# A new order of the loading phase, first weight columns as fp32 on the hardware queue, attention weights transposed by DMA

## The chip, the cores and the metric

The kernel runs on one core of one Trainium2 chip. A core has five engines with a queue of instructions each: PE (TensorE, matmuls; its weight loads are listed as PEld), DVE (VectorE), ACT (ScalarE), POOL (GpSimd) and SP (SyncE, which here only issues DMAs). Instructions of one engine start in order; between engines they wait on semaphores. The metric is the time of one execution on the device in microseconds (us).

## What is computed

Two stages. First a small cross attention between `x` (8 batches, 8 heads, 512 rows, 64 columns) and a `state` of 32 rows per head, in both directions; then a gated linear layer over all rows:

```
scores  = x @ state^T / 8 ;  a  = softmax over the 32 state rows ;  xread = a @ state
scores2 = state @ x^T / 8 ;  a2 = softmax over the 512 rows of x ;  sread = a2 @ x
rows    = concat(xread, sread) with heads side by side          (4352 rows of 512)
out     = (sigmoid(rows @ w_gate) * (rows @ w_val)) @ w_out     (512 -> 1536 -> 512)
```

The kernel never forms `xread`. With SW = state @ w (per batch, for both weights) the first product of the layer is a @ SW, so the normalized attention weights, transposed, go straight into the large matmuls.

## The kernel before

It is written under a manual schedule: the order in which the code issues instructions is the order in each engine's queue.

Names. `xf` is x of a batch in fp32, `xb` in bf16 (two buffers), `xT` its transpose. `sTz` is the state, transposed and padded with zeros so that a pair of heads shares one matmul. `Sp` are the scores in PSUM, `E` their Exp. `rs`, `ri`, `ab` are row sums, reciprocals and normalized weights (`at_norm`, half a batch at a time); `aT` is `ab` transposed: eight PE transposes and a copy on DVE (`at_aT`). `Eb` is E in bf16, cast by POOL, for the other direction (`at_sr`, tiles `srp`, results in `XS`). `sw_visit` makes SW for a range of weight columns in PSUM tiles `swp` (four buffers), and `sw_evac` takes the oldest of them to SBUF, on the engines named. `gv(b, f)` makes 128 gate and 128 val columns of batch b (four matmuls of 512 columns into two `gvp` tiles), then Tanh on ACT (`th`) and the gating product on DVE (`glu`). `out_mm(b, k)` is four matmuls of the last product; every third call ends in a copy to `res` and a store on SP's queue. `warm` issues matmuls without use, to keep PE active.

The program has two phases.

- Loading. State and x of batches 0 and 1 come on SP's queue. The weights, x of batch 2 and `w_out` come on POOL's queue, which casts weights to bf16 on the way; columns 0 to 255 first, then 256 to 511, 512 to 1023, 1024 to 1535. Batches 0 and 1 go through attention (with PE transposes of x), and all 24 of their `gv` are made here, in the hand-written list `order`, with one evacuation on ACT and one on DVE after each entry. The state copies are made in two portions: `sTz` of batches 0 and 1 early, of batches 2 to 7 later, four copies on ACT.
- The loop. In iteration b, step f of twelve issues `out_mm(b-1, f)` and, from b=2 on, `gv(b, f)`. Beside that it prepares batch nb = b+1: SW at steps 0, 4 and 8 with one evacuation a step, scores at steps 2 and 3, `at_norm` at 4 and 5, `at_aT` at 7, `at_sr` at 8. The x of batch nb+1 is cast on POOL and transposed by four DMAs on SP's queue (`at_xT_dma`). There are two `gvp` buffers, so one `gv` is in flight at a time.

An iteration with `gv`, as the code issues it:

```
            if nb is not None:
                if f % 4 == 0:
                    sw_visit(nb, f * 128, 512, 0, 1)
                sw_evac(act)
                ...
                elif f == 4:
                    at_norm(nb, 0, nc.vector)
                    at_Eb(nb)
```

Of the kernel before, what the change touches and what calls it, by code (L numbers as in the profile page):

```python
# [16 lines left out]
def kernel(  # L17
# [58 lines left out]
    def load_w(lo, n):  # L76
        for w, src in ((wg, moe_w_gate), (wv, moe_w_val)):
            nc.gpsimd.dma_start(w[:, :, lo:lo + n], src.rearrange("(k p) n -> p k n", p=128)[:, :, lo:lo + n])
# [16 lines left out]
    def at_xT_pe(b, i, place, cps):  # L95
        ps = place[0].tile((128, 2, 4, 128), BF, name="xTp", tag=place[1])
# [13 lines left out]
    def at_S(b, i, place):  # L110
        if i == 0:
            E1s[b] = ap_.tile((128, 4, 2, 4, Ns), FP, name="E1")
        ps = place[0].tile((128, 4, 2, 2, Ns), FP, name="Sp", tag=place[1])
        for jj in range(2):
            for c in range(4):
                nc.tensor.matmul(ps[:, c, :, jj], xTs[b][:, 2 * i + jj, c], sTz[:, b, 2 * i + jj], start=True, stop=True)  # L116
        nc.scalar.activation(E1s[b][:, :, :, 2 * i:2 * i + 2].rearrange("p c e j n -> p (c e) j n"),  # L117
                             ps.rearrange("p c e j n -> p (c e) j n"), AF.Exp, scale=scale)
# [6 lines left out]
    def at_norm(b, i, eng):  # L125
        if i == 0:
            abs_[b] = ap_.tile((128, 4, 2, 128), BF, name="ab")
        E = E1s[b][:, :, :, 2 * i:2 * i + 2].rearrange("p c e j n -> p (c e) j n")
        rs = ap_.tile((128, 8, 2), FP, name="rs")
        nc.vector.tensor_reduce(rs, E, AX.X, ALU.add)  # L130
        ri = ap_.tile((128, 8, 2), FP, name="ri")
        nc.vector.reciprocal(ri, rs)  # L132
        eng.tensor_tensor(abs_[b].rearrange("p c e (j n) -> p (c e) j n", n=Ns)[:, :, 2 * i:2 * i + 2], E,  # L133
                          ri.unsqueeze(3).to_broadcast((128, 8, 2, Ns)), ALU.mult)

    def at_aT(b, place, cps):
        ps = place[0].tile((128, 2, 4, 128), BF, name="aTp", tag=place[1])
        for e in range(2):
            for c in range(4):
                nc.tensor.transpose(ps[:, e, c], abs_[b][:, c, e], ident)  # L140
        aTs[b] = ap_.tile((128, 2, 512), BF, name="aT")
        m = 2 // len(cps)
        for i, cp in enumerate(cps):
            cp(aTs[b][:, i * m:i * m + m], ps[:, i * m:i * m + m].rearrange("p g c t -> p g (c t)"))

    def at_sr(b, place):
# [7 lines left out]
        for j in range(4):  # L154
            for c in range(4):
                nc.tensor.matmul(sr[:, j], xbs[b][:, c, 2 * j:2 * j + 2].rearrange("p h d -> p (h d)"),  # L156
                                 Eb[:, c, :, j], start=(c == 0), stop=(c == 3))
        r2 = ap_.tile((128, 4, Ns), FP, name="r2")
# [7 lines left out]
    sw_left = []  # L166

    def sw_mm(pss, b, w, lo, n, o):
        for j in range(4):
            for e in range(2):  # L170
                rows = slice(e * 64, (e + 1) * 64)
                nc.tensor.matmul(pss[e][j * Ns:(j + 1) * Ns, o:o + n], sTz[rows, b, j, e],  # L172
                                 (wg, wv)[w][rows, j, lo:lo + n], start=True, stop=True)

    def sw_visit(b, lo, n, *ws):
# [3 lines left out]
        if not ws:  # L179
# [3 lines left out]
            for e in range(2):  # L183
                sw_left.append((SWs[b][:, e, :, lo:lo + n], pss[e].rearrange("p (w n) -> p w n", w=2)))
        for w in ws:
            pss = [p_sw.tile((128, 512), FP, name="swp", tag="swp")[:, :n] for e in range(2)]
            sw_mm(pss, b, w, lo, n, 0)
            for e in range(2):
                sw_left.append((SWs[b][:, e, w, lo:lo + n], pss[e]))

    def sw_evac(*cps):
        for cp in cps:
            if sw_left:
                cp(*sw_left.pop(0))  # L194


    def gv(b, f, place=None):
        place = place or (p_gv, "gv")
# [4 lines left out]
        pss = []
        for w in range(2):
            ps = place[0].tile((128, 512), FP, name="gvp", tag=place[1])[:, :n]
            if b < B:
                for g in range(2):
                    nc.tensor.matmul(ps, SWs[b][:, g, w, fs], aTs[b][:, g], start=(g == 0), stop=(g == 1))  # L208
# [4 lines left out]
        th = fp.tile((128, 512), FP, name="th")[:, :n]  # L213

        nc.scalar.activation(th, pss[0], AF.Tanh, scale=0.5)  # L215
        nc.vector.scalar_tensor_tensor(glus[b][:, f], th, 1.0, pss[1], ALU.add, ALU.mult)  # L216
# [50 lines left out]
    load_x(1, nc.sync)  # L267
    make_identity(nc, ident)
# [154 lines left out]
```

## Time and profile before

| | us |
|---|---|
| median of 3 runs (lowest, highest) | 248.19 (247.83, 249.14) |
| the profiled execution, whole | 247.92 |
| its span | 246.1 |
| loading, to the first output matmul | 53.0 |
| one iteration of the loop, b=2 to 6 | 25.43 |
| busy PE / DVE / ACT / POOL | 229.8 / 128.4 / 139.2 / 36.4 |

All rows of the profile are of that one execution, and times in it count from the start of its span. The row of a stretch gives its borders and length, then busy time and number of instructions of PE, PEld, DVE, ACT and POOL, the clock granted to TensorE (1.00 is full speed), the busy share of the DMA engines and GB/s. The row of a timeline gives start, duration, engine, line, operation, output <- input, and in brackets the idle time before it and what ended that. A row of a group gives its count, busy time and mean duration in ns, and the idle time before it with its releasers. PE's durations overlap: matmuls are pipelined, so the cost of one is the distance from start to start.

### The profile page before, as it was taken

What the parts mean: (1) busy time and instruction counts of PE and PEld (TensorE: products, weight loads), DVE (VectorE), ACT (ScalarE), POOL (GpSimd) and SP (SyncE); (2) the same over time, 40 slices, a digit from 0 to 9 for tenths busy, and PEclk for the clock granted to TensorE, in tenths of its full rate; (3) what the DMA queues carried; (4) which work ended last, traced back from release to release, by engine and by line L of the source; (5) the groups of instructions that cost most, each with busy time, mean ns of one, the idle gap of its engine ahead of it and who ended that gap; (6) DMA issues with size and microseconds to landing.
All of it is one profiled execution on the core that took longest, in us unless ns stands there. A gap on an engine that the chain in (4) does not pass through costs nothing.

```text
span 246.1 us, 4632 instructions
## 1 busy us (share of the span) xinstructions
PE 229.8 (93%) x1828; PEld 114.4 (46%) x1828; DVE 128.4 (52%) x210; ACT 139.2 (57%) x258; POOL 36.4 (15%) x68
## 2 busy tenths in 40 slices
PE   7674999999999999999999999999999999999993
PEld 6651443444544444444443544354445444466643
DVE  2768488965325853485338633854375444332300
ACT  4756367666567556764686467647764734433311
POOL 1796020003304000320013000400020000000000
PEclk9998699999999999999999999999999999999999
DMA  6999996601364516242533444331111111111113
GB/s 226 260 174 207 284 206 78 195 3 43 97 156 176 120 53 187 73 107 64 147 112 87 87 103 153 86 89 45 43 44 45 43 43 43 45 59 69 45 33 96
DMA packets 31734, 25.99 MB, mean 106 GB/s; under 512 B 14048, under 2 KB 27104, under 8 KB 31712
## 3 DMA queue, kind: packets, MB, share of 16 engines
q1 hardware_dynamic: 25488, 19.80, 27.9%
q0 software_dynamic: 6080, 5.77, 13.6%
q8 instruction: 14, 0.23, 0.4%
q10 hardware_dynamic: 144, 0.13, 0.2%
q14 instruction: 8, 0.07, 0.1%
HBM read 18.35 MB, written 8.91 MB: 111 GB/s over the span
## 4 chain that ended last, share of the span: by engine, by line
PE 76%; DVE 13%; issue 4%; ACT 4%; DMA 2%; SPq 0%; ACTq 0%; DVEq 0%
PE outp L229 30%; PE gvp L208 29%; PE swp L172 5%; DVE glu L216 4%; PE gvp L211 4%; DVE rs L130 3%; DVE ab L133 3%; PE srp L153 2%; PE aTp L140 2%; ACT th L215 2%; DMA sf<-in_state_dram 2%; PE srp L156 2%; DVE ri L132 1%; PE Sp L116 1%; ACT E L117 1%
## 5 line engine op out<-in xcount | busy, mean ns | idle before, releaser
L216 DVE SCALAR_TENSOR_TENSOR glu<-th,gvp 128x512 bf16<-128x512 f32 (+1 forms) x108 | 70.9, 656 | 87.7 <-ACT th L215 63.9
L208 PE MATMUL gvp<-aT,SW 128*128 128x512 bf16 x384 | 100.6, 384 | 6.1 <-DVE glu L216 2.5
L229 PE MATMUL outp<-wo,glu 128*128 128x512 bf16 x396 | 100.0, 379 | 0.0
L215 ACT ACTIVATE th<-gvp 128x512 f32<-128x512 f32 (+1 forms) x108 | 61.8, 572 | 59.6 <-PE gvp L208 49.8
L208 PEld LDWEIGHTS <-SW 128*128 128x128 bf16 x384 | 36.7, 98 | 53.1 <-issue 7.9
L229 PEld LDWEIGHTS <-glu 128*128 128x128 bf16 x396 | 36.2, 98 | 41.2 <-issue 4.8
L194 ACT CAST SW<-swp 128x512 bf16<-128x512 f32 (+1 forms) x85 | 48.7, 581 | 7.9 <-PE swp L172 7.1
L233 ACT ACTIVATE res<-outp 128x512 f32<-128x512 f32 x33 | 19.7, 597 | 25.9 <-PE outp L229 23.5
L123 POOL CAST Eb<-E 128x256 bf16<-128x256 f32 x32 | 12.3, 428 | 123.8 <-ACT E L117 123.8
L87 POOL CAST xb<-xf 128x1024 bf16<-128x1024 f32 (+1 forms) x14 | 14.3, 1045 | 19.0 <-PE srp L156 13.0
L133 DVE TENSOR_TENSOR ab<-E,ri 128x512 bf16<-128x512 f32 x16 | 15.8, 989 | 0.5
L130 DVE TENSOR_REDUCE rs<-E 128x16 f32<-128x512 f32 x16 | 10.8, 677 | 4.0 <-ACT E L117 4.0
L172 PE MATMUL swp<-wv,sTz 64*32 64x512 bf16 (+1 forms) x208 | 11.2, 366 | 0.0
L172 PEld LDWEIGHTS <-sTz 64*32 64x32 bf16 x416 | 4.6, 89 | 14.0 <-issue 13.8
L172 PE MATMUL swp<-wg,sTz 64*32 64x512 bf16 (+1 forms) x208 | 10.6, 374 | 0.5 <-DVE glu L216 0.5
L117 ACT ACTIVATE E<-Sp 128x512 f32<-128x512 f32 x16 | 9.8, 613 | 1.5 <-PE Sp L116 1.5
L159 DVE RECIPROCAL r<-srp 128x128 f32<-128x128 f32 x8 | 7.7, 956 | 5.1 <-PE srp L156 5.1
L116 PE MATMUL Sp<-sTz,xT 128*128 128x64 bf16 x128 | 6.5, 193 | 2.5 <-DVE sTz L296 1.1
L116 PEld LDWEIGHTS <-xT 128*128 128x128 bf16 x128 | 5.8, 98 | 6.3 <-DVE sTz L296 1.2
L194 DVE CAST SW<-swp 128x512 bf16<-128x512 f32 (+1 forms) x13 | 8.3, 643 | 0.3 <-PE swp L172 0.2
L262 PE MATMUL warm<-ident 128*128 128x128 bf16 x80 | 7.0, 261 | 1.4 <-POOL ident masks.py:199 1.4
L211 PE MATMUL gvp<-XS,wv 128*128 128x256 bf16 x48 | 7.2, 272 | 0.1
(45 smaller groups left out, 102.0 us busy)
## 6 DMA issues: line engine op xcount, KB each, us to landing
out_dram<-res SPq DMA_DIRECT2D x31, 256.0 KB, 2.3
xf<-in_x_dram SPq DMA_DIRECT2D x6, 1024.0 KB, 6.7
wo<-in_moe_w_out_dram POOLq DMA_DIRECT2D x3, 512.0 KB, 19.0
xf<-in_x_dram SPq DMA_DIRECT2D x2, 512.0 KB, 5.4
wg<-in_moe_w_gate_dram POOLq DMA_DIRECT2D x2, 512.0 KB, 10.3
wv<-in_moe_w_val_dram POOLq DMA_DIRECT2D x2, 512.0 KB, 11.8
xf<-in_x_dram POOLq DMA_DIRECT2D x1, 1024.0 KB, 15.8
sf<-in_state_dram SPq DMA_DIRECT2D x1, 512.0 KB, 3.9
```

What stands on the lines that cost most here:

```text
L87: cp(xbs[b].rearrange("p c h d -> p h c d")[:, lo:lo + n], xfs[b][:, lo:lo + n])
L116: nc.tensor.matmul(ps[:, c, :, jj], xTs[b][:, 2 * i + jj, c], sTz[:, b, 2 * i + jj], start=True, stop=True)
L130: nc.vector.tensor_reduce(rs, E, AX.X, ALU.add)
L133: eng.tensor_tensor(abs_[b].rearrange("p c e (j n) -> p (c e) j n", n=Ns)[:, :, 2 * i:2 * i + 2], E, ri.unsqueeze(3).to_broadcast((128, 8, ...
L172: nc.tensor.matmul(pss[e][j * Ns:(j + 1) * Ns, o:o + n], sTz[rows, b, j, e], (wg, wv)[w][rows, j, lo:lo + n], start=True, stop=True)
L194: cp(*sw_left.pop(0))
L208: nc.tensor.matmul(ps, SWs[b][:, g, w, fs], aTs[b][:, g], start=(g == 0), stop=(g == 1))
L211: nc.tensor.matmul(ps, (wg, wv)[w][:, j, fs], XS[:, j], start=(j == 0), stop=(j == 3))
L215: nc.scalar.activation(th, pss[0], AF.Tanh, scale=0.5)
L216: nc.vector.scalar_tensor_tensor(glus[b][:, f], th, 1.0, pss[1], ALU.add, ALU.mult)
L229: nc.tensor.matmul(ops[b, c], glus[b][:, f, c * 128:(c + 1) * 128], wo[:, f], start=(f == 0), stop=(f == NF - 1))
L233: nc.scalar.activation(res, ops[b, c], AF.Copy, scale=0.5)
```

## The change

It does five things.

1. The loading phase is one flat list of calls with a searched order. For that the helpers are cut into their parts: `xT_mm` and `xT_cp`, `S_mm` and `S_exp`, `n_sum` (sum and reciprocal) and `n_mul` (product), `aT_mm` and `aT_cp`, `sr_mm` and `sr_fin`, `gv_mm`, `gv_th` and `gv_glu`; `sw_cp` evacuates a named tile on a named engine. Two of the four products of loading go to POOL. PE's matmuls of `warm` go from 80 to 56.
2. Columns 0 to 255 of both weights come as fp32 on SP's queue behind x of batch 1 and are cast to bf16 by DVE (gate) and POOL (val). POOL's own loads start after a one-column copy that waits for x of batch 1 (`gate`).
3. The state is cast and copied once, without padding, into `sTc`, from which `sw_visit` now reads; POOL makes `sTz` from it, for batches 1 and 0 early and 2 to 7 at the end of loading.
4. `aT` of batches 2 to 7 is made by four DMA transposes on SP's queue (`aT_dma`) instead of PE and DVE, and its layout is (row block, pair, row), so that PE reads it in four pieces.
5. In the loop, scores are made at steps 0 and 1, sums at 1 and 3, products at 2 and 4, the other direction at 5; x is loaded one batch further ahead.

The core of the diff:

```diff
+    def gate():
+        nc.gpsimd.tensor_copy(pre[:, 1:2], xfs[1][:, 0, 0, 0:1])
+    def cast_w(w, cp):
+        cp((wg, wv)[w][:, :, 0:256], wfs[w])
...
+    def aT_dma(b):
+        for c in range(4):
+            nc.sync.dma_start_transpose(aT_tile(b)[:, c], abs_[b][:, c].rearrange("p e k -> p (e k)"))
...
-                nc.tensor.matmul(pss[e][j * Ns:(j + 1) * Ns, o:o + n], sTz[rows, b, j, e],
+                nc.tensor.matmul(pss[e][j * Ns:(j + 1) * Ns, o:o + n], sTc[rows, b, j],
...
-                    nc.tensor.matmul(ps, SWs[b][:, g, w, fs], aTs[b][:, g], start=(g == 0), stop=(g == 1))
+                    nc.tensor.matmul(ps, SWs[b][:, g, w, fs], aTs[b][:, :, g], start=(g == 0), stop=(g == 1))
...
+    for src in (moe_w_gate, moe_w_val):
+        wf = wp.tile((128, 4, 256), FP, name="wf", bufs=2)
+        nc.sync.dma_start(wf, src.rearrange("(k p) n -> p k n", p=128)[:, :, 0:256])
+        wfs.append(wf)
...
-    sb = wp.tile((128, 16, 2, D), BF, name="sb")
-    nc.vector.tensor_copy(sb[:, :, 0], sf)
-    nc.scalar.copy(sb[:, :, 1], sf)
+    sb = wp.tile((128, 16, D), BF, name="sb")
+    nc.vector.tensor_copy(sb[:, 0:8], sf[:, 0:8])
+    nc.scalar.copy(sb[:, 8:16], sf[:, 8:16])
...
+    def pad(b, n=1):
         for e in range(2):
             rows = slice(e * 64, (e + 1) * 64)
+            nc.gpsimd.tensor_copy(sTz[rows, b:b + n, :, e], sTc[rows, b:b + n])
...
+    sr_mm(0, OU)
+    gv_th(1, 5)
...
+    pad(2, 6)
     cast_x(2, pool, 0, 4)
     cast_x(2, pool, 4, 4)
     at_xT_dma(2)
+    load_x(3, nc.sync)
...
+                lo, q = f // 4 * 512, f % 4
+                if q == 0:
+                    sw_visit(nb, lo, 512, 0, 1)
+                sw_cp(nb, lo, q // 2, q % 2, act)
+                if f < 2:
+                    S_mm(nb, f, AT)
+                    S_exp(nb, f)
                 elif f == 5:
+                    sr_mm(nb, AT)
+                    sr_fin(nb)
...
+                if f in (1, 3):
+                    n_sum(nb, f // 2)
+                elif f in (2, 4):
+                    n_mul(nb, f // 2 - 1, nc.vector)
+                if f == 2:
+                    at_Eb(nb)
+                    if nb + 2 < B:
+                        load_x(nb + 2, nc.sync)
+                elif f == 4:
+                    aT_dma(nb)
```

How the order moves, at three places. First ACT's queue in loading, from the Exp of batch 0's second half on; `E_194` and `E_339` are the Exp tiles of batches 0 and 1. Before:

```order
L117 ACTIVATE E_194<-Sp 128x8x64
L87 CAST xb<-xf 128x4x4x64
L103 COPY xT<-xTp 128x1024
L144 COPY aT<-aTp 128x512
L194 CAST SW<-swp 128x256
L117 ACTIVATE E_339<-Sp 128x8x64
L194 CAST SW<-swp 128x256
L215 ACTIVATE th<-gvp 128x512
L117 ACTIVATE E_339<-Sp 128x8x64
L215 ACTIVATE th<-gvp 128x512
L296 COPY sTz<-stp 64x24x2x8 x4
L194 CAST SW<-swp 128x2x256 x2
```

After, with `E_232` and `E_314` for batches 0 and 1:

```order
L99 CAST xb<-xf 128x4x4x64
L135 ACTIVATE E_232<-Sp 128x8x64
L119 COPY xT<-xTp 128x1024 x2
L135 ACTIVATE E_314<-Sp 128x8x64
L232 CAST SW<-swp 128x256 x2
L135 ACTIVATE E_314<-Sp 128x8x64
L232 CAST SW<-swp 128x256 x2
L232 CAST SW<-swp 128x2x256 x2
L256 ACTIVATE th<-gvp 128x512
L232 CAST SW<-swp 128x2x256 x2
```

The four state copies are gone from ahead of the double-width evacuations, and all evacuations of the first columns are on ACT.

Second, DVE's queue in iteration b=2, which prepares batch 3. Before:

```order
L216 SCALAR_TENSOR_TENSOR glu<-th,gvp 128x512 x5
L130 TENSOR_REDUCE rs<-E_1143 128x16
L132 RECIPROCAL ri<-rs 128x16
L133 TENSOR_TENSOR ab<-E_1143,ri 128x8x64
L216 SCALAR_TENSOR_TENSOR glu<-th,gvp 128x512
L130 TENSOR_REDUCE rs<-E_1143 128x16
L132 RECIPROCAL ri<-rs 128x16
L133 TENSOR_TENSOR ab<-E_1143,ri 128x8x64
L216 SCALAR_TENSOR_TENSOR glu<-th,gvp 128x512 x2
L144 COPY aT<-aTp 128x1024
L216 SCALAR_TENSOR_TENSOR glu<-th,gvp 128x512
L159 RECIPROCAL r_1356<-srp 128x128
```

After:

```order
L261 SCALAR_TENSOR_TENSOR glu<-th,gvp 128x512 x2
L148 TENSOR_REDUCE rs<-E_1111 128x16
L150 RECIPROCAL ri<-rs 128x16
L261 SCALAR_TENSOR_TENSOR glu<-th,gvp 128x512
L156 TENSOR_TENSOR ab<-E_1111,ri 128x8x64
L261 SCALAR_TENSOR_TENSOR glu<-th,gvp 128x512
L148 TENSOR_REDUCE rs<-E_1111 128x16
L150 RECIPROCAL ri<-rs 128x16
L261 SCALAR_TENSOR_TENSOR glu<-th,gvp 128x512
L156 TENSOR_TENSOR ab<-E_1111,ri 128x8x64
L261 SCALAR_TENSOR_TENSOR glu<-th,gvp 128x512
L199 RECIPROCAL r_1268<-srp 128x128
```

A `glu` now stands between each sum and its product, and the copy of `aT` is gone.

Third, SP's queue at the beginning of the loop. Before, after the transposes of batch 2:

```order
L73 DMA xf<-in_x_dram 128x8x256
L235 DMA out_dram<-res 128x512 x2
L108 DMA_TRANSPOSE xT<-xb 128x4x128 x4
L235 DMA out_dram<-res 128x512 x2
L73 DMA xf<-in_x_dram 128x8x256
L235 DMA out_dram<-res 128x512 x2
```

After:

```order
L78 DMA xf<-in_x_dram 128x8x256
L280 DMA out_dram<-res 128x512
L78 DMA xf<-in_x_dram 128x8x256
L177 DMA_TRANSPOSE aT<-ab 128x2x128 x4
L280 DMA out_dram<-res 128x512
L124 DMA_TRANSPOSE xT<-xb 128x4x128 x4
L280 DMA out_dram<-res 128x512 x3
```

Four transposes of `aT` come ahead of the next batch's transposes of x, with one output store between them.

More of the change, by code (lines that the diff above doesn't have):

```diff
@@ L136, in at_aT, with halfE @@
[L136 to L146, printed above, removed]
+    def halfE(b, i):
+        return E1s[b][:, :, :, 2 * i:2 * i + 2].rearrange("p c e j n -> p (c e) j n")
@@ new lines, in aT_mm, with aT_tile, aT_cp @@
+    def aT_mm(b, place):
+        ps = held["aT", b] = place[0].tile((128, 4, 2, 128), BF, name="aTp", tag=place[1])
+        for c in range(4):
+            for e in range(2):
+                nc.tensor.transpose(ps[:, c, e], abs_[b][:, c, e], ident)
+    def aT_tile(b):
+        if b not in aTs:
+            aTs[b] = ap_.tile((128, 4, 2, 128), BF, name="aT")
+        return aTs[b]
+    def aT_cp(b, i, cp):
+        cs = slice(0, 4) if i is None else slice(2 * i, 2 * i + 2)
+        cp(aT_tile(b)[:, cs], held["aT", b][:, cs])
@@ L150, in at_sr @@
-        sm = ps[:, 256:384].rearrange("p (j n) -> p j n", j=4)
+        held["sr", b] = place[0].tile((128, 512), FP, name="srp", tag=place[1])
+        sr, sm = sr_parts(b)
         for e in range(2):
@@ new lines @@
+    xT_cp(0, 1, 1, act)
+    xT_cp(0, 1, 0, vec)
+    cast_x(1, vec, 0, 4)
+    S_mm(0, 0, SWP)
+    S_exp(0, 0)
+    warm(12, SWP)
+    gate()
+    load_w(0, 256, 256)
+    S_mm(0, 1, AT)
+    cast_x(1, act, 4, 4)
+    n_sum(0, 0)
+    xT_mm(1, 0, OU)
+    load_w(1, 256, 256)
+    load_w(0, 512, 512)
+    S_exp(0, 1)
+    cast_w(0, vec)
+    n_sum(0, 1)
+    xT_mm(1, 1, SWP)
+    xT_cp(1, 0, None, act)
+    xT_cp(1, 1, None, act)
+    n_mul(0, 1, nc.vector)
+    S_mm(1, 0, GV)
+    sw_visit(0, 0, 256, 0)
```

332 lines of the change are left out of this document (211 added, 121 removed).

## The prediction

> **What bounds the kernel now.** I read first the page's slices of the granted clock of TensorE, then stretches of the trace cut where the program changes: loading (0 to 53.01), the iteration b=1 (to 67.7) and the five iterations b=2 to 6.
>
> ```profile
> PEclk9998699999999999999999999999999999999999
> ```
> ```profile
> core 0: us, PE busy (x) PEld busy (x) DVE busy (x) ACT busy (x) POOL busy (x), PEclk, DMA share, GB/s
> 16.93:20.84 3.91, 3.27 (x56) 1.29 (x48) 2.24 (x4) 3.46 (x8) 3.40 (x9) 1.00 1.24 206
> 20.84:24.87 4.03, 0.63 (x7) 0.10 (x1) 3.84 (x8) 1.71 (x4) 1.43 (x3) 0.69 1.24 207
> 24.87:29.34 4.47, 4.46 (x31) 1.89 (x32) 1.71 (x3) 1.19 (x2) 0.00 (x0) 0.51 1.14 307
> 29.34:53.01 23.67, 23.67 (x201) 10.19 (x193) 21.10 (x35) 16.27 (x29) 2.02 (x2) 1.00 0.73 138
> ...
> 67.70:194.90 127.20, 124.65 (x964) 57.15 (x963) 68.86 (x109) 81.39 (x152) 15.04 (x28) 1.00 0.34 96
> ```
>
> From 29.34 on PE nearly always has work (23.67 of 23.67 us, then 124.65 of 127.20). Before that it has not: from 20.84 to 24.87 it works 0.63 of 4.03 us, and from 24.87 to 29.34 it works at a granted clock of 0.51. The timeline of that place says why:
>
> ```profile
> 16.43 0.37 ACT L194 CAST SW<-swp 128x256 bf16<-128x256 f32 x1
> ...
> 16.93 0.60 PE L208 MATMUL gvp<-aT,SW 128*128 128x512 bf16 x2
> ...
> 19.57 1.92 ACT L296 COPY sTz<-stp 64x384 bf16<-64x384 bf16 x4
> ...
> 21.52 1.07 ACT L194 CAST SW<-swp 128x512 bf16<-128x512 f32 x2
> ...
> 22.64 0.61 PE L208 MATMUL gvp<-aT,SW 128*128 128x512 bf16 x1 [1.78 <-ACT SW L194]
> 22.93 0.69 DVE L133 TENSOR_TENSOR ab<-E,ri 128x512 bf16<-128x512 f32 x1
> ...
> 23.54 1.28 DVE L194 CAST SW<-swp 128x512 bf16<-128x512 f32 x2
> ...
> 24.88 1.46 PE L208 MATMUL gvp<-aT,SW 128*128 128x512 bf16 x3 [1.62 <-DVE SW L194]
> ...
> 29.34 2.76 PE L208 MATMUL gvp<-aT,SW 128*128 128x512 bf16 x12
> ```
>
> PE waits for evacuations of SW. On ACT they stand behind the state copies (1.92 us), on DVE, busy 3.84 of 4.03 us, behind batch 1's normalization. Between 16.93 and 29.34 only 16 of these matmuls ran, four gv; the fifth gv is the first of the x12 group and ends at about 30.2.
>
> **Part 1, loading.** New are a searched order, the first 256 columns of both weights as fp32 on SP's queue, and state copies without padding. The prices, first from loading, then from the loop:
>
> ```profile
> 0.00:5.00 5.00, 3.64 (x35) 3.65 (x36) 1.28 (x2) 1.85 (x3) 1.04 (x10) 1.00 0.58 193
> 5.00:10.00 5.00, 3.06 (x51) 2.45 (x50) 2.50 (x7) 3.14 (x7) 2.31 (x4) 1.00 1.02 333
> ```
> ```profile
> 7.69 0.61 POOL L87 CAST xb<-xf 128x512 bf16<-128x512 f32 x1 [6.04 <-DMA xf<-in_x_dram]
> ...
> 8.24 0.88 POOL L78 DMA_DIRECT2D wg<-in_moe_w_gate_dram  x1
> ...
> 8.54 0.41 PE L116 MATMUL Sp<-sTz,xT 128*128 128x64 bf16 x8 [1.06 <-DVE sTz L296]
> ...
> 10.77 2.18 DVE L133 TENSOR_TENSOR ab<-E,ri 128x512 bf16<-128x512 f32 x1
> ...
> 11.31 1.09 POOL L87 CAST xb<-xf 128x1024 bf16<-128x1024 f32 x1
> ```
> ```profile
> L208 PE MATMUL gvp<-aT,SW 128*128 128x512 bf16 x48 | 12.6, 379 | 0.6 <-DVE glu L216 0.6
> ...
> L216 DVE SCALAR_TENSOR_TENSOR glu<-th,gvp 128x512 bf16<-128x512 f32 x12 | 8.2, 685 | 10.6 <-ACT th L215 8.6 <-PE Sp L116 1.2 <-PE gvp L208 0.8
> ...
> L194 ACT CAST SW<-swp 128x512 bf16<-128x512 f32 x12 | 7.0, 584 | 0.5 <-PE swp L172 0.4
> ...
> L130 DVE TENSOR_REDUCE rs<-E 128x16 f32<-128x512 f32 x2 | 1.4, 675 | 0.0
> ...
> L116 PE MATMUL Sp<-sTz,xT 128*128 128x64 bf16 x16 | 0.8, 193 | 0.0
> ...
> L156 PE MATMUL srp<-Eb,xb 128*128 128x64 bf16 x16 | 0.6, 193 | 0.0
> ...
> L132 DVE RECIPROCAL ri<-rs 128x16 f32<-128x16 f32 x2 | 0.5, 252 | 0.1
> ```
>
> I walk the new order with such durations, each instruction starting when its engine and its inputs are ready. State and two batches are 2.62 MB; 5 us at 193 GB/s and 5 at 333 make 2.63 MB, so x of batch 1 is there just before 10. The two fp32 blocks (0.52 MB each, 1.6 us at 333 GB/s) land near 11.4 and 13.0.
>
> POOL casts its x until 8.3, then makes four small padded copies (0.25 each, an estimate, well below its cast of 0.61 for four times the columns on twice the partitions), so the first scores start at 9.4 instead of 8.54. It issues three weight loads (0.8 each, to 12.2), normalizes half a batch (`n_mul`) to 13.3 and casts the val block (1.09) to 14.4. ACT carries xT copies, a cast of x and three Exp to 14.7, two evacuations of 256 columns (0.37 each), the fourth Exp and two more evacuations, to 16.75. So the first gv starts at 16.8, as before (16.93): neither the early weights nor the compact copies help that point.
>
> The gain comes right after it. No state copy and no second normalization stands ahead of the evacuations: ACT does two for batch 1, one Tanh (taken like an evacuation, 0.6) and two more by 19.8, DVE two by 20.6. PE runs the second gv at 19.2 and then without long gaps; its fifth gv ends at 22.7, against 30.2. The visits of columns 0 to 511 are done at both points, and what is left is the same: 19 gv, eight half-visits and two sr. That took 53.01 - 30.2 = 22.8 us before. DVE was busy 21.10 of 23.67 us there, so it holds PE back little. Loading then ends at 45.5, 7.5 us earlier.
>
> What the trace of before has no row for is `n_mul` on POOL, with two inputs. Its bounds are 0.61 (POOL's cast of that size) and 2.18 (the slowest product on DVE); I took 1.1, nearer to the cast. The Trainium skill, GPSIMD Engine Reference, Engine selection, says that two-input elementwise work takes about twice as long on GpSimd as on VectorE. By it the price would be an estimated 1.4 us, and the sum 0.3 us worse.
>
> DVE's 2.18 us at 10.77 is mostly a wait beside POOL's DMA issue and cast; the product at 22.93 takes 0.69. The new order puts more POOL work beside DVE, so I take 1.0 us off the walk (0 to 2.5: one or two such waits). **Loading: -6.5 us** (-7.5 to -5.0).
>
> At no cost: the two wide padded copies for batches 2 to 7, which POOL makes while it would be idle (2.02 of 23.67 us busy); and wo, whose 3 MB come last as before and are used only when loading ends.
>
> **Part 2, the loop.** One period of 25.43 us, from 103.50 to 128.93 (the second group of rows above is from it):
>
> ```profile
> 105.11 1.45 DVE L133 TENSOR_TENSOR ab<-E,ri 128x512 bf16<-128x512 f32 x1
> ...
> 106.05 5.14 SPq L108 DMA_TRANSPOSE xT<-xb  x4
> ...
> 109.85 0.61 PE L140 MATMUL aTp<-ident,ab 128*128 128x128 bf16 x8
> ...
> 110.29 1.03 PE L229 MATMUL outp<-wo,glu 128*128 128x512 bf16 x4
> ...
> 111.16 1.03 PE L208 MATMUL gvp<-aT,SW 128*128 128x512 bf16 x4
> ...
> 112.11 0.41 PE L172 MATMUL swp<-wg,sTz 64*32 64x512 bf16 x8
> ...
> 112.67 0.62 PE L153 MATMUL srp<-Eb,ones 128*128 128x128 bf16 x8
> ```
>
> From start to start, eight transposes take 110.29 - 109.85 = 0.44 us of PE, an output step 0.87, a visit 0.56. The transposes leave PE. PE's 0.6 us of waiting for glu comes from sum, reciprocal and product (0.68 + 0.25 + 1.45, the last with POOL's cast beside it) standing together between two glu. Now sum and product stand in different steps: 0.69 + 0.93 and 0.69 + about 0.7 fit into a step of 2 x 0.87 = 1.74 us. POOL's cast can still hold one product; I leave 0.2 us of the wait. So -0.84 a period (-1.04 if nothing is left, -0.4 if the wait stays), five times: **-4.2** (-5.2 to -2.0). DVE's copy of aT goes too, but nothing waited for it.
>
> aT is now read by PE in four pieces instead of one. Of the rows above, S (L116) reads one piece of 64 columns and sr (L156) two of 32: 193 ns both, so nothing is charged.
>
> In SP's queue four aT transposes stand ahead of output stores and of the next xT transposes. An xT issue takes 5.14 / 4 = 1.29 us; aT is half as wide, so between 0.64 and 1.29. Counted from a period's start, the products end at 12.3, aT's issues at most at 17.4, xT's at 22.9, with the landing of the last at about 24.2. The scores need it at 24.6 + 2.4 = 27.0. That leaves 2.8 us, and no charge.
>
> **Part 3, the seam.** The cast and transposes of batch 2 wait for sr of batch 0, which the search put late:
>
> ```profile
> 35.23 2.02 POOL L87 CAST xb<-xf 128x1024 bf16<-128x1024 f32 x2 [12.97 <-PE srp L156]
> ...
> 37.29 6.32 SPq L108 DMA_TRANSPOSE xT<-xb  x4
> ```
> ```profile
> 19.30:22.70 3.40, 1.16 (x34) 0.50 (x33) 2.88 (x6) 3.23 (x7) 2.96 (x8) 0.96 1.24 207
> ```
>
> Cast, issue and about 1.2 us for the last landing take 9.5 us, or 8.4 with issues of 1.29. On PE seven gv (6.1), an output step (0.87) and a visit (0.56), 7.5 us, lie between. So the scores of batch 2, no longer at the third step of b=1 but at the first, wait 0.9 to 2.0 us, which is new. The transposes of aT(2) may also push back xT(3). Against it 0.44 us of transposes go. **Seam: +0.5** (0 to +2).
>
> Sum: -6.5 - 4.2 + 0.5 = -10.2. The profiled execution took 247.92, the median of the runs is 248.19; from the median that is 238.0.
>
> **Rivals.**
> - The clock falls again. Before, it fell late in the last row above, a stretch with 1.16 us of PE work in 3.40, and stayed near 0.5 through 24.87 to 29.34 although PE was full: about 6.8 us in all. The new program drops 24 of 80 warming matmuls, and its work from 10 to 19 us is short pieces. If 6.8 us of dense work ran at 0.5, it would cost 3.4 us: 241.4. Against it: in my walk each 3.4 us there hold at least 2.4 us of PE work. The Trainium skill, TensorE: Matmul & The Clock Gate, Part 4, says that transposes do not count as busy for this gate. By that rule the xT and aT transposes would not hold the clock, which speaks for this rival; no row of before tests it alone.
> - POOL is slow at its new work, and both `n_mul` take 2.18 or more: aT comes 2 us later, 240.0.
> - The loop gains nothing, since another wait takes the place of the one for glu (DVE at sr, or the single score buffer, now used in neighbouring steps): 238.0 + 4.2 = 242.2. In the walk the tightest place has 0.1 us to spare.
> - Slower: a transpose of aT holds SP so long that xT is late in each period. Past the 2.8 us of slack each us of lateness costs a us, five times. To lose the 10.2 and 1.2 more, 2.3 a period are needed, so the four must take 5.1 + 2.8 + 2.3 = 10.2, or 2.6 us each: twice xT's issue for half its data. It would end above 249.4.
>
> **Chances.** About 0.5% (1.2 us) is what a measurement here can tell from no change. Forecast 0.60 (235 to 239.9), clock 0.13, slow POOL 0.11, no gain in the loop 0.08, slower 0.04; mixtures near no change 0.04. From the same cases: faster 0.92, same 0.03, slower 0.05. The range reaches from the full gain of loading and loop (-7.5 - 5.2 = -12.7, about 235.5) less 1 us for the walk's own error, 234.5, up to 243.0, which takes in the clock, POOL and loop cases.
>
> **What would show it.** Right: the fifth gv ends before 24 and the first output matmul starts between 45 and 48; PEclk shows no fall after 15; aT transposes take about 1 us each on SP; periods of 24.4 to 24.8. Wrong: PEclk of 0.5 in the dense stretch; PE waiting for SW or aT between 17 and 23; a wait of the scores for xT in every period; or DVE, nearly full in loading, pacing the gv at more than 0.9 us each.

## The result and the profile after

The changed kernel takes 237.12 us (median of 4 runs, 235.75 to 239.31) against 248.11 for the kernel before on the same chip. The ratio is 0.9532, 95% interval [0.9468, 0.9596]. The run at 239.31 was in a slower state of the chip and is not in the ratio; the runs in it have a mean of 236.7. The profiled execution took 238.31 us, with a span of 236.5.

First the slices of the granted clock, on the page of the kernel after. Apart from the last slice, the only fall is in slice 12, at about 65 us, where the kernel before had none:

```profile
PEclk9999999999979999999999999999999999999998
```

Then the windows of the same places as before, cut where the new loading phase ends, and 109 us of the loop:

```profile
core 0: us, PE busy (x) PEld busy (x) DVE busy (x) ACT busy (x) POOL busy (x), PEclk, DMA share, GB/s
16.92:20.84 3.92, 2.88 (x47) 1.34 (x47) 3.85 (x6) 2.86 (x7) 3.90 (x8) 1.00 1.17 179
20.84:24.87 4.03, 3.37 (x23) 1.29 (x20) 3.78 (x7) 2.98 (x6) 4.03 (x8) 1.00 1.18 179
24.87:45.71 20.84, 20.79 (x181) 9.71 (x182) 18.09 (x30) 15.02 (x28) 4.75 (x6) 1.00 1.25 223
75.00:184.00 109.00, 107.89 (x814) 49.54 (x826) 58.18 (x94) 72.41 (x134) 13.04 (x22) 1.00 0.37 97
```

From 20.84 to 24.87 PE works 3.37 us instead of 0.63, at full clock. DVE is busy nearly all of both early stretches (3.85 of 3.92, 3.78 of 4.03), and so is POOL (3.90 and 4.03). The wait that PE has left there, 1.04 us at 19.81, ends with a product on DVE, so DVE is the likelier pace of the start. The PE timeline shows this wait and the marks that the prediction named:

```profile
16.92 1.06 PE L246 MATMUL gvp<-aT,SW 128*128 128x512 bf16 x4
...
19.81 0.61 PE L163 MATMUL aTp<-ident,ab 128*128 128x128 bf16 x8 [1.04 <-DVE ab L156]
20.25 3.62 PE L246 MATMUL gvp<-aT,SW 128*128 128x512 bf16 x16
23.80 0.41 PE L212 MATMUL swp<-wg,sTc 64*32 64x512 bf16 x8
...
45.71 1.03 PE L274 MATMUL outp<-wo,glu 128*128 128x512 bf16 x3
```

The first gv starts where it did (16.92). The x16 group ends with the fifth gv at 23.8, where the next matmul starts; before, the fifth gv ended at about 30.2. The first output matmul comes at 45.71 instead of 53.01.

In the loop the group of gv matmuls shows no wait for glu any more (one period, 84.88 to 109.07; before, it had 0.6 us of it):

```profile
L246 PE MATMUL gvp<-aT,SW 128*128 128x512 bf16 x48 | 12.4, 379 | 0.0
```

The two executions, cut at starts of ACT's copies to `res` (the 4th ends iteration b=1, the 8th b=2, the 24th b=6):

| stretch | before | after | difference |
|---|---|---|---|
| loading, to the first output matmul | 53.01 | 45.71 | -7.3 |
| from there to copy 4 (b=1) | 15.15 | 14.01 | -1.1 |
| copies 4 to 8 (b=2) | 24.52 | 27.78 | +3.3 |
| copies 8 to 24 (b=3 to 6) | 101.20 | 96.73 | -4.5 |
| copy 24 to the end of the span | 52.2 | 52.3 | +0.1 |

The sum is -9.5; the spans differ by 9.6. One row has the wrong sign. The timeline there, first SP's queue and then PE:

```profile
52.03 5.05 SPq L177 DMA_TRANSPOSE aT<-ab  x4
57.18 0.53 SPq L280 DMA_DIRECT2D out_dram<-res  x1
57.80 6.16 SPq L124 DMA_TRANSPOSE xT<-xb  x4
```
```profile
64.63 0.24 PE L130 MATMUL Sp<-sTz,xT 128*128 128x64 bf16 x1 [2.54 <-DMA xT<-xb]
65.11 0.45 PE L130 MATMUL Sp<-sTz,xT 128*128 128x64 bf16 x5 [0.25 <-DMA xT<-xb]
```

The scores of batch 3 wait 2.8 us for xT, whose four DMAs stood in SP's queue behind the four of aT(2). PE stood empty, and then the clock fell for some 3 us, in which PE was soon full again (slices of 1 us):

```profile
65.00:66.00 1.00, 0.67 (x6) 0.55 (x8) 0.00 (x0) 0.34 (x1) 0.00 (x0) 0.50 0.92 342
66.00:67.00 1.00, 1.00 (x3) 0.30 (x2) 0.00 (x0) 0.26 (x1) 0.00 (x0) 0.50 0.59 182
67.00:68.00 1.00, 1.00 (x4) 0.39 (x3) 0.00 (x0) 0.00 (x0) 0.00 (x0) 0.50 0.00 0
```

### The profile page after: what moved, and what is told of

Read it like the earlier page. It is cut to its first block, busy times and chain, and to the rows that moved or that the text cites. A ratio compares the mean times of both kernels' runs of the same rounds, so it can differ in the third digit from the quotient of the medians.

```text
span 236.5 us, 4542 instructions
## 1 busy us (share of the span) xinstructions
PE 220.2 (93%) x1749; PEld 110.5 (47%) x1772; DVE 120.6 (51%) x197; ACT 138.9 (59%) x258; POOL 43.1 (18%) x75
## 4 chain that ended last, share of the span: by engine, by line
PE 82%; DMA 9%; SPq 2%; POOL 2%; issue 2%; ACT 1%; DVE 0%; DVEq 0%; ACTq 0%; POOLq 0%
PE outp L274 35%; PE gvp L246 33%; PE swp L212 5%; PE gvp L249 4%; DMA wv<-in_moe_w_val_dram 4%; DMA xf<-in_x_dram 3%; SPq L124 2%; PE srp L193 2%; PE srp L190 2%; PE Sp L130 2%; DMA xT<-xb 1%; DMA out_dram<-res 1%; POOL wg L83 1%; POOL wv L90 1%; ACT res L278 1%
## 5 line engine op out<-in xcount | busy, mean ns | idle before, releaser
L274 PE MATMUL outp<-wo,glu 128*128 128x512 bf16 x373 | 97.1, 381 | 1.9 <-issue 1.0
L246 PE MATMUL gvp<-aT,SW 128*128 128x512 bf16 x384 | 96.9, 380 | 0.1
L232 ACT CAST SW<-swp 128x512 bf16<-128x512 f32 (+1 forms) x90 | 50.4, 579 | 7.0 <-PE swp L212 6.2
L99 POOL CAST xb<-xf 128x1024 bf16<-128x1024 f32 (+1 forms) x13 | 15.1, 1183 | 11.8 <-DMA xf<-in_x_dram 11.8
L156 DVE TENSOR_TENSOR ab<-E,ri 128x512 bf16<-128x512 f32 x14 | 14.9, 1067 | 0.1
L212 PE MATMUL swp<-wv,sTc 64*32 64x512 bf16 (+1 forms) x208 | 10.0, 361 | 0.9 <-DMA wv<-in_moe_w_val_dram 0.7
L212 PE MATMUL swp<-wg,sTc 64*32 64x512 bf16 (+1 forms) x208 | 10.3, 369 | 0.1
L212 PEld LDWEIGHTS <-sTc 64*32 64x32 bf16 x416 | 4.2, 89 | 11.5 <-issue 10.1
L249 PE MATMUL gvp<-XS,wg 128*128 128x256 bf16 x48 | 7.2, 272 | 0.1
L307 PE MATMUL warm<-ident 128*128 128x128 bf16 x56 | 5.5, 280 | 1.4 <-POOL ident masks.py:199 1.4
```

The costliest lines, as they stand in the source:

```text
L99: cp(xbs[b].rearrange("p c h d -> p h c d")[:, lo:lo + n], xfs[b][:, lo:lo + n])
L212: nc.tensor.matmul(pss[e][j * Ns:(j + 1) * Ns, o:o + n], sTc[rows, b, j], (wg, wv)[w][rows, j, lo:lo + n], start=True, stop=True)
L232: cp(*sw_left.pop((b, lo, w, e)))
L246: nc.tensor.matmul(ps, SWs[b][:, g, w, fs], aTs[b][:, :, g], start=(g == 0), stop=(g == 1))
L249: nc.tensor.matmul(ps, (wg, wv)[w][:, j, fs], XS[:, j], start=(j == 0), stop=(j == 3))
L274: nc.tensor.matmul(ops[b, c], glus[b][:, f, c * 128:(c + 1) * 128], wo[:, f], start=(f == 0), stop=(f == NF - 1))
```

## The experiments

Every ratio below is to the kernel before, run on the same chip (medians 247.58, 248.25 and 248.05 in the three groups of four kernels). Since the chips differ, two kernels are best compared by their ratios: 0.001 is 0.25 us.

**1. aT by one DMA** (the changed kernel, else unchanged):

```diff
-        for c in range(4):
-            nc.sync.dma_start_transpose(aT_tile(b)[:, c], abs_[b][:, c].rearrange("p e k -> p (e k)"))
+        nc.sync.dma_start_transpose(aT_tile(b).rearrange("p c e t -> p (c e) t"),
+                                    abs_[b].rearrange("p c e k -> p (c e k)"))
```

> Edit: the changed kernel, but aT of a batch is made by one DMA transpose of eight 128x128 blocks instead of four of two blocks. Theory: a DMA transpose holds SP for about 1.25 us whatever its width (aT with two blocks 1.24, xT with four 1.27), so in b=1 the four of aT hold back the four of xT(3) by 5.05 us, PE waits 3.2 us for them at the scores of batch 3 and then runs 3.4 us at half clock. With one aT transpose xT(3) is issued 3.8 us earlier: no wait there, no fall of the clock, 232.5 to 234.5 us. Rival 1: the issue goes by the data; one wide transpose holds SP for about 5 us, xT(3) is as late as before, 237. Rival 2: the wait is for something else (cast, load of x), no change, 237.

Measured: 233.21 us, ratio 0.9412 [0.9385, 0.9438]. SP's queue and the PE timeline at the same place, and the window 59.50 to 75.00 (in the kernel after, PE worked 12.33 of these 15.50 us, at a clock of 0.89):

```profile
51.53 1.56 SPq L176 DMA_TRANSPOSE aT<-ab  x1
53.19 0.66 SPq L280 DMA_DIRECT2D out_dram<-res  x1
53.94 6.10 SPq L124 DMA_TRANSPOSE xT<-xb  x4
```
```profile
61.37 0.41 PE L130 MATMUL Sp<-sTz,xT 128*128 128x64 bf16 x8
```
```profile
59.50:75.00 15.50, 15.50 (x133) 7.28 (x132) 9.74 (x16) 10.62 (x20) 3.86 (x6) 1.00 0.63 171
```

The scores wait no more and the clock does not fall there. Iteration b=2 takes 23.20 us (copies 4 to 8) instead of 27.78, so the wait and what hung on it cost 4.6 us of the profiled execution: 2.8 us of waiting, and about 1.7 for 3.4 us at half clock. That execution, 238.31, was a long one. By the ratios the gain is 3.0 us (0.9532 to 0.9412); the medians differ by 3.9.

**2. aT by two DMAs** of four blocks each (`for i in range(2)`, over `2 * i:2 * i + 2`):

> The changed kernel with aT transposed by two DMAs of four blocks each instead of four of two. Theory A (a transposing DMA costs SP about 1.24 us whatever its width, and batch 3's xT is late by what aT's issues take beyond the slack): aT takes 2.5 us of SP instead of 5.05, xT(3) is late by at most 0.3 us instead of 2.8, the clock does not fall behind it: 233.3 to 234.3, as with one DMA. Rival B (the price goes with the data, and the single DMA is a form of its own): 2.4 us each, 5 in all, 236.5 to 237.5.

Measured: 232.63 us, 0.9381 [0.9357, 0.9404], no wait of the scores: theory A, though a little faster than its range. The tile's rows in the kernel after, with one DMA and with two (number of issues: shortest/median/longest ns on SP):

```profile
L177 SPq DMA_TRANSPOSE aT<-ab x24: 1168/1241/1652, 52.0 to 176.1; - x24
```
```profile
L176 SPq DMA_TRANSPOSE aT<-ab x6: 1237/1242/1927, 51.5 to 167.3; - x6
```
```profile
L177 SPq DMA_TRANSPOSE aT<-ab x12: 1189/1257/2072, 51.5 to 168.4; - x12
```

An issue costs SP 1.24 to 1.26 us whether it moves two, four or eight blocks of 128x128. The intervals of two DMAs and of one overlap; both beat the changed kernel.

**3. aT on PE** (PE transposes and the copy on DVE at step 7 again; the new steps kept):

```diff
-                elif f == 4:
-                    aT_dma(nb)
+                elif f == 7:
+                    aT_mm(nb, AT)
+                    aT_cp(nb, None, vec)
```

> Edit: the changed kernel, but aT of batches 2 to 7 is made by eight PE transposes and a DVE copy at step 7 of the loop, as in the kernel before. Theory: each period gets longer by the 0.44 us of transposes (24.2 to about 24.65, no wait for glu), while the seam gets shorter, since nothing stands ahead of xT(3) on SP: no wait at the scores of batch 3, no fall of the clock. 6 x 0.44 = +2.6, seam -3.3 to -5: 234.5 to 236.5. Rival: most of the shorter period comes from the transposes and their copy on DVE, not from the split of sums and products: period 25.0 or more, 238 or more in all.

Measured: 236.23, 0.9534 [0.9506, 0.9561]. A period is 24.63 us, from SP's load of x at 90.71 to that at 115.34:

```profile
90.71 0.43 SPq L78 DMA_DIRECT2D xf<-in_x_dram  x1
...
115.34 0.43 SPq L78 DMA_DIRECT2D xf<-in_x_dram  x1
```

That is 0.4 more than with the DMAs (24.2), and it has no wait at batch 3. The two cancel: with four DMAs, moving aT off PE brought nothing on balance.

**4. The old steps** (scores at steps 2 and 3, `n_sum` and `n_mul` together at 4 and 5, sr at 8; aT by four DMAs kept):

> Edit: the changed kernel, but the loop's steps are those of the kernel before (scores at 2 and 3, sum and product of a half together at 4 and at 5, sr at 8, transposes of x at 7); aT stays on DMA. Theory: PE waits for glu again, 0.6 us a period, so the period is about 24.8 against 24.2 (4 to 5 times, +2.5 to +3); the scores of batch 3 come two steps later, so the wait at the seam (3.2 us and the clock) goes or shrinks: 234.5 to 238. Rival: without the transposes in it, the place has slack enough, the period stays at 24.2 and the time is 232 to 234.

Measured: 238.82, 0.9628 [0.96, 0.9656], slightly above what was expected. The period is 24.99 us (copies 8 to 12). The wait for glu is back (waits of PE from 40 to 200: us in all, times, longest):

```profile
PE gvp L246 <- DVE glu L261: 2.5, 9, 0.3
```

From 25.43 the DMA takes 0.44, to 24.99, and the steps 0.8, to 24.2.

**5. The old loading** before the new loop:

> Edit: the loading phase of the kernel before (its order, weights, state copies; only the layout of aT is the new one) with the loop of the changed kernel. Theory: loading ends at 53.0 instead of 45.7 and the rest is that of the changed kernel, so 237.1 + 7.3 = 244.4 (243 to 246). Rival: what the new loading gained is partly given back in the seam (x of batch 3 and its transposes come late because loading is short); then with the long loading the seam costs nothing, and the time is 240 to 242.

Measured: 244.04, 0.9863 [0.9826, 0.99], with the first output matmul at 52.65. So the new loading is worth 6.9 us by that mark and by the medians, and 8.2 by the ratios. The scores of batch 3 wait here too:

```profile
PE Sp L116 <- DMA xT<-xb: 3.0, 2, 2.4
```

So that wait does not come from the shorter loading.

The next four each undo one part of the new loading, starting from experiment 1 (233.21, 0.9412).

**6. First weight columns on POOL's queue**, cast on the way, without the fp32 tiles and their two casts (`load_w(0, 0, 256)` and `load_w(1, 0, 256)` issued where the pads and casts of x are):

> Edit: the kernel with one aT transpose, but the first 256 columns of both weights come on POOL's queue again, cast on the way and issued right after POOL's cast of x of batch 0; the fp32 tiles and their casts on DVE and POOL go. Theory: between x of batch 1 (10.5) and the dense stretch (20.2) the chain of waits runs through DVE, and the gate cast (0.69) is a link of it; without it the dense stretch starts 0.7 us earlier if x of batch 1 is not later, but the weights now share the DMA engines with that x and delay it by up to 1.5 us. So between -0.7 and +0.8: 232.5 to 234, against 233.2. Rival: early weights on the hardware queue are what makes the loading short; without them the first evacuations and gv come 2 us later or more, 235 to 236.

Measured: 233.73, 0.9412 [0.9384, 0.944]. The ratio is that of experiment 1: the hardware queue brings nothing that can be measured.

**7. State copies on ACT**: the two wide padded copies for batches 2 to 7 on ACT, ahead of its first evacuations of 512 columns, instead of `pad(2, 6)` on POOL.

> Edit: the kernel with one aT transpose, but the two wide padded copies of the state (batches 2 to 7) are made by ACT directly ahead of the first double-width evacuations, not by POOL at the end of loading. Theory: this puts back the work that stood there in the kernel before (1.9 us), and PE waits for these evacuations: 1.3 to 1.9 us slower, 234.5 to 235.1. Rival: the evacuations are not last there, since batch 1's product and its transposes on PE come no earlier; then at most 0.5 us, 233.2 to 233.7.

Measured: 234.09, 0.9431 [0.9405, 0.9458]. ACT's timeline shows the copies where the prediction had seen the fault of the old program:

```profile
17.30 1.68 ACT L403 COPY sTz<-sTc 64x768 bf16<-64x768 bf16 x2
19.00 1.07 ACT L232 CAST SW<-swp 128x512 bf16<-128x512 f32 x2
```

By the ratios they cost about half a microsecond (0.9412 to 0.9431), less than the 1.3 to 1.9 that were expected if PE waited for these evacuations.

**8. Without the small warming groups** (`warm(12)` and `warm(8)` left out):

> Edit: the kernel with one aT transpose, without the 12 and the 8 warming matmuls between 9 and 15 us. Theory: they only keep the clock; PE has 3.2 us of work in each 5 us there, so most of it stays at full clock, and a fall there hits a stretch that DVE paces: 0 to +0.7, 233.2 to 233.9. Rival (the clock rival of the prediction): without them the clock falls to 0.5 into the dense stretch for up to 3.4 us, +1 to +2: 234.2 to 235.2.

Measured: 233.82, 0.942 [0.9394, 0.9445]. Windows of loading:

```profile
10.00:15.00 5.00, 3.51 (x49) 2.67 (x47) 4.08 (x8) 4.13 (x6) 3.71 (x5) 0.58 0.94 238
15.00:20.00 5.00, 4.38 (x64) 2.18 (x64) 4.58 (x7) 3.61 (x9) 4.98 (x8) 0.50 1.18 150
```

The same place in the profile of experiment 1, from which this one starts:

```profile
10.00:15.00 5.00, 4.74 (x72) 4.31 (x68) 4.32 (x8) 4.43 (x6) 4.03 (x5) 0.66 1.03 245
15.00:20.00 5.00, 3.25 (x78) 1.63 (x75) 4.82 (x8) 4.08 (x11) 4.98 (x8) 1.00 1.13 154
```

The clock is low for ten microseconds instead of 3.4, and the time hardly changes. The likely reason is that PE has waits to spare there, while DVE is busy 4.58 of 5.00 us. The gain of the new loading is therefore not the clock in its first 20 us. The fall of 3.4 us says the same: experiments 1 to 4 keep the whole new loading, all four have it at 9 to 13.5 us, and they reach the first output matmul at 45.1 to 45.8; the profile of the changed kernel has none there and reaches it at 45.71.

**9. Both `n_mul` of POOL on DVE:**

> Edit: the kernel with one aT transpose, but the two products of loading that POOL made (1.07 us each) are made by DVE. Theory: DVE's own products beside them take 1.76 and 1.88 us instead of 0.69, since POOL holds them up; with all four on DVE the pair takes 2 x 0.69 = 1.4, so each pair ends 0.3 to 0.5 us earlier: -0.5 to -1, 232.2 to 232.7. Rival: DVE is busy nearly all the time there, so two more products of 0.69 make its chain longer, and the waits come from POOL's other work (casts, DMA issue) all the same: +0.5 to +1.4, 233.7 to 234.6.

Measured: 233.9, 0.9424 [0.9398, 0.9449]. No gain and no clear loss. The two pairs of products, now on DVE alone and still beside other work of POOL:

```profile
14.17 2.33 DVE L156 TENSOR_TENSOR ab<-E,ri 128x512 bf16<-128x512 f32 x2
18.84 2.03 DVE L156 TENSOR_TENSOR ab<-E,ri 128x512 bf16<-128x512 f32 x2
```

The last three take the kernel before and change its loading by hand. What they turn on is when aT of batch 1 is made.

**10. Evacuations first:**

```diff
     gv(0, 1, SWP)
+    sw_visit(1, 0, 256)
+    sw_evac(act, vec)
+    sw_visit(0, 256, 256)
+    sw_evac(act, vec)
+    gv(0, 2, SWP)
     sT_copy(0, slice(2, B), act)
     at_norm(1, 0, nc.vector)
...
-    order = [(sw_visit, 1, 0, 256), (sw_visit, 0, 256, 256), (gv, 0, 2), (at_aT, 1, AT, (vec,)), (gv, 0, 3),
+    order = [(at_aT, 1, AT, (vec,)), (gv, 0, 3),
...
-    n_gv = 0
+    n_gv = 1
```

> The kernel before, with one thing moved in loading: the visits of columns 0 to 255 of batch 1 and 256 to 511 of batch 0, their four evacuations and the third gv are issued ahead of the late state copies (ACT) and of batch 1's normalization (DVE). Theory A, the prediction's step (PE stood still from 20.8 to 24.9 because evacuations were queued behind state copies and normalization): evacuations end at about 21 to 22.2 instead of 24.8, PE goes on from there, the clock does not fall: -3 to -5 us, 243 to 245. Rival B (batch 1's normalization itself is what comes too late, since only two gv can run without aT of batch 1; moving it back only moves the wait to aT(1), at about 26): -1 to +1 us, 247 to 249.2, with PE waiting for ab or aT near 24 to 26.

Measured: 249.15, 1.0027 [1.0003, 1.0052]: rival B. The evacuations end at 22.8, PE makes its third gv, and then waits for batch 1's weights:

```profile
22.71 0.82 PE L208 MATMUL gvp<-aT,SW 128*128 128x512 bf16 x3 [0.69 <-ACT SW L194]
27.95 1.03 PE L140 MATMUL aTp<-ident,ab 128*128 128x128 bf16 x8 [4.41 <-DVE ab L133]
```

The profiled execution was the slowest of the twelve (250.38), and 1.2 us late at the first gv already (18.09 against 16.93), ahead of the edit.

**11. Batch 1 early:**

```diff
     at_S(1, 0, AT)
+    at_S(1, 1, OU)
     sw_visit(0, 0, 256, 1)
     sw_evac(act, vec)
+    at_norm(1, 0, nc.vector)
     gv(0, 0, SWP)
-    at_S(1, 1, OU)
     gv(0, 1, SWP)
+    at_norm(1, 1, nc.vector)
+    sw_visit(1, 0, 256)
+    sw_evac(act, vec)
+    sw_visit(0, 256, 256)
+    sw_evac(act, vec)
+    at_aT(1, AT, (vec,))
+    gv(0, 2, SWP)
     sT_copy(0, slice(2, B), act)
-    at_norm(1, 0, nc.vector)
     sT_copy(1, slice(2, B), act)
-    at_norm(1, 1, nc.vector)
...
-    order = [(sw_visit, 1, 0, 256), (sw_visit, 0, 256, 256), (gv, 0, 2), (at_aT, 1, AT, (vec,)), (gv, 0, 3),
+    order = [(gv, 0, 3),
...
-    n_gv = 0
+    n_gv = 1
```

> The kernel before, reordered by hand in loading: both scores of batch 1 follow the first half-visit, its normalization stands on DVE ahead of the two glu and of the evacuations of batch 1's first and batch 0's second columns, its transposes ahead of the third gv, the late state copies on ACT behind all that. Theory A (batch 1's attention came too late): aT(1) is there at about 23 instead of 27, PE is dense from about 22.5 with a clock that falls shortly or not at all: -2 to -4 us, 244 to 246. Rival B (the order of these few instructions matters little as DVE has the same work ahead of the fifth gv, and the gain came from elsewhere): -0.8 to +0.8 us, 247.3 to 249.

Measured: 245.51, 0.9895 [0.9867, 0.9924]: theory A.

```profile
21.28 0.62 PE L140 MATMUL aTp<-ident,ab 128*128 128x128 bf16 x8 [1.24 <-DVE ab L133]
...
49.69 1.03 PE L229 MATMUL outp<-wo,glu 128*128 128x512 bf16 x4
```
```profile
20.84:24.87 4.03, 3.01 (x15) 1.32 (x16) 2.87 (x5) 1.92 (x5) 1.33 (x3) 0.74 1.25 208
24.87:29.34 4.47, 4.47 (x40) 1.54 (x39) 2.98 (x5) 3.59 (x7) 0.00 (x0) 0.85 1.17 291
```

The same instructions in another order bring the first output matmul 3.3 us forward, although the clock falls here too: 4.03 x 0.26 + 4.47 x 0.15 is up to another 1.7 us lost, an estimate that takes PE as full. The edit moves batch 1's attention, two visits with their evacuations and the state copies at once, so it does not say which of them counts.

**12. Warm in the gap** (`warm(40)` ahead of the third and of the fourth gv of the kernel before):

> The kernel before with 40 more warming matmuls ahead of its third and of its fourth gv, which fill the two stretches in which PE stood still between 20.8 and 24.9; nothing else is changed. Theory A (the cold clock costs: 4.47 us of full PE at 0.51 from 24.87 to 29.34): -1.5 to -2.3 us, 245.8 to 246.6, granted clock 1.00 from 24 to 30. Rival B (DVE or an evacuation paces the gv there, so a cold PE costs little, as in the run without small warming matmuls): -0.6 to +0.3 us, 247.5 to 248.5, with the clock held all the same.

Measured: 248.31, 1.0004 [0.9982, 1.0026]. This decides nothing. The clock held at 1.00 from 22 to 30, but the second group stood in the way of the fourth gv:

```profile
25.31 0.61 PE L140 MATMUL aTp<-ident,ab 128*128 128x128 bf16 x8
25.75 2.40 PE L262 MATMUL warm<-ident 128*128 128x128 bf16 x40
28.20 0.81 PE L208 MATMUL gvp<-aT,SW 128*128 128x512 bf16 x3
```

Its 2.40 us are as much as the better clock was to bring (4.47 x 0.49 = 2.2). One small group ahead of the third gv alone would have been the test.

Over all the profiles, the start of batch 1's aT and that of the first output matmul:

| kernel | aT(1) on PE | first output matmul | between |
|---|---|---|---|
| evacuations first (10) | 27.95 | 55.5 | 27.5 |
| before | 26.13 | 53.01 | 26.9 |
| warm in the gap (12) | 25.31 | 52.95 | 27.6 |
| old loading (5) | 25.15 | 52.65 | 27.5 |
| batch 1 early (11) | 21.28 | 49.69 | 28.4 |
| weights on POOL's queue (6) | 21.08 | 46.13 | 25.1 |
| products on DVE (9) | 20.93 | 45.99 | 25.1 |
| no small warming (8) | 20.79 | 45.95 | 25.2 |
| state copies on ACT (7) | 20.47 | 45.71 | 25.2 |
| one DMA (1) | 20.18 | 45.22 | 25.0 |
| two DMAs (2) | 20.08 | 45.13 | 25.1 |
| aT on PE (3) | 20.04 | 45.16 | 25.1 |
| old steps (4) | 20.02 | 45.83 | 25.8 |
| after | 19.81 | 45.71 | 25.9 |

From the old loading to the new the two go together. Inside a group they need not: with the old loading (5) aT(1) is 1.0 us earlier than in the kernel before, and the first output matmul only 0.4.

## Why the prediction was right or wrong

The forecast, 238.0, was right within 1 us, in part by luck: loading and loop gave more than was said, the seam took it back. Of the signs named for being right, the fifth gv and the first output matmul came where they were said to. The periods, 24.2, were shorter than 24.4 to 24.8, an issue of aT took 1.24 us instead of about 1, and PEclk did fall after 15. One sign of being wrong showed too: PE waited for aT of batch 1 between 17 and 23, 1.04 us at 19.81.

- **Loading, -6.5 predicted, -7.3 measured.** Right: the first gv unmoved, the fifth before 24, the first output between 45 and 48. The walk was 1.1 us early at the fifth gv (22.7 against 23.8), about the discount that I took off it. The remaining stretch was a little shorter than before instead of equal (21.9 against 22.8 us). Half wrong was the cause. I put PE's wait down to evacuations behind state copies *and* normalization. Experiment 7 puts state copies back ahead of evacuations and loses only half a microsecond; in experiment 10 earlier evacuations alone gain nothing, since PE then waits for batch 1's normalization, without which only a few gv can run. Counted to the start of aT(1), 6.3 of the 7.3 us are gained by then (26.13 to 19.81), and 1.0 after it. Moving batch 1's attention and those evacuations forward together in the old program (11) gained 2.5 us of run time. The rest of the 7.3 is located, but not shown by an experiment: no single part of the new loading that I undid was worth more than 0.5 us by the ratios, which leave about 0.9 us either way.
  The stretch behind aT(1), 25.9 us in the new order and 28.4 in experiment 11, can be added up in the traces, from the start of each matmul to the next. The visits make 1.9 of the 2.5 us: 4.3 us of PE in experiment 11 against 2.4, since sixteen narrow matmuls of them were still to come (0.6), and the 64 of 512 columns took 58 ns each instead of 38. The gv take 0.3 more although four fewer matmuls were left, part of them at the low clock. Why the wide visits cost more in the old order was not tested.
- **`n_mul` on POOL, 1.1 taken, 1.07 measured.** The Trainium skill, GPSIMD Engine Reference, Engine selection, gives about twice VectorE's time for two-input work, from which I had estimated 1.4; against the undisturbed 0.69 of DVE the factor here is 1.55. As I had expected, the price came on DVE: its own products ran long beside POOL's work, by 1.07 and 1.20 us, and PE's wait of 1.04 us at 19.81 is for the second.

```profile
13.60 1.76 DVE L156 TENSOR_TENSOR ab<-E,ri 128x512 bf16<-128x512 f32 x1
13.74 1.07 POOL L156 TENSOR_TENSOR ab<-E,ri 128x512 bf16<-128x512 f32 x1
...
17.78 1.89 DVE L156 TENSOR_TENSOR ab<-E,ri 128x512 bf16<-128x512 f32 x1
```

- **Loop, -0.84 a period predicted, -1.23 measured** (25.43 to 24.20), and past the -1.04 that I had called the most. The transposes gave the 0.44 of my working. The steps were mis-sized: I counted 0.4 of a wait of 0.6, and they gave 0.8 (experiment 4). The wait itself was larger than I read it. Its two places in the period of the kernel before:

```profile
106.36 0.59 PE L208 MATMUL gvp<-aT,SW 128*128 128x512 bf16 x2
107.21 0.59 PE L208 MATMUL gvp<-aT,SW 128*128 128x512 bf16 x2 [0.26 <-DVE glu L216]
107.64 1.02 PE L229 MATMUL outp<-wo,glu 128*128 128x512 bf16 x4
108.50 0.59 PE L208 MATMUL gvp<-aT,SW 128*128 128x512 bf16 x2
109.42 0.59 PE L208 MATMUL gvp<-aT,SW 128*128 128x512 bf16 x2 [0.32 <-DVE glu L216]
```

  Undelayed, a pair of these matmuls costs 0.43 us from start to start (107.21 to 107.64). Here the second pairs start 0.85 and 0.92 us after the first, so PE lost 0.42 + 0.49 = 0.91 us. The brackets show only 0.58 of it, because they count from the end of a matmul, whose duration of 379 ns overlaps the next. In the kernel after, one gv of a period takes 1.13 instead of 1.03 us (0.1 lost), and 0.91 - 0.1 is the 0.8; with the old steps (experiment 4) both losses are back. The row of the kernel after:

```profile
97.07 1.13 PE L246 MATMUL gvp<-aT,SW 128*128 128x512 bf16 x4
```

- **Seam, +0.5 predicted, for the wrong batch.** I said that scores of batch 2 would wait, since their cast stood behind sr of batch 0. They did not. The cast took the buffer of batch 1, whose sr the search had put first, and it waited for its load only (in the kernel after, sr of batch 1 starts on PE at 29.38, that of batch 0 at 38.62):

```profile
33.54 2.02 POOL L99 CAST xb<-xf 128x1024 bf16<-128x1024 f32 x2 [5.89 <-DMA xf<-in_x_dram]
```

  I had mentioned that aT(2) might push xT(3), and charged nothing. That was the failing step: it cost 4.6 us of the profiled execution, 3.0 by the ratios. My slack of 2.8 us was worked out for a full iteration of 24.6 us. Iteration b=1 has no gv and lasts 14, and the chain through SP's queue is as long there: 5.05 for aT, a store, and 6.16 for xT. Without the wait this place would have gained: -1.1 in b=1, of which 0.44 are the transposes, and PE's wait of 0.6 us for the score buffer there, which is gone. The surplus of the loop and of loading paid for the seam.
- **Rivals.** The clock did fall, though not in the dense stretch of loading but behind the wait at 65 us; in the profiles of experiments 1 to 4 and 6 to 9 it also fell ahead of the dense stretch, where it cost nothing that shows (experiment 8). "The loop gains nothing" and "POOL is slow" fell. The slower case needed 2.6 us for each transpose of aT; it took 1.24. Its resource, SP's queue, was the right one all the same: it decided at one place rather than in every period.

## What to carry to other kernels

Work out a queue's slack separately for the shortest iteration, where a chain of DMA issues is as long as elsewhere and the cover is not. If issues have a fixed price, give each DMA all the data that is ready: about 1.24 us for eight blocks instead of 5.0 was worth 3.0 to 3.9 us here. Measure a wait of pipelined matmuls from start to start, not by the idle time that a row shows. When an engine stands idle behind a busy queue, ask which result it can't go on without; moving another entry of that queue forward (experiment 10) only moves the wait.

## What was not expected of the hardware

- A transposing DMA in SBUF cost SP 1.24 to 1.26 us (medians) for 128x256, 128x512 and 128x1024 bf16 alike. The estimate that it might go with width (0.64 for half) was wrong.
- After some 3 us nearly without PE work, the granted clock stood at 0.50 for about 3 us of full work, in the middle of a program that kept 1.00 elsewhere up to its last microseconds.
- A DVE product of 0.69 us took 1.76 and 1.89 us in the kernel after while POOL worked beside it. With both products of a pair on DVE, the pairs took 2.33 and 2.03 us, so sharing them with POOL shortened a pair by 0.57 and 0.14 us only, and the run times do not tell the two apart.
